# Gated linear attention into a two-layer feed-forward, one core: another order of the same work, and the last unit's second layer in two column halves

## The chip, the cores and the metric

The kernel runs on one core of one Trainium2 chip. The metric is the device time of one execution in microseconds (us). A core has five engines that run at once, each through its own list of instructions in the order of the program: TensorE (PE: matrix products; PEld is its weight load), VectorE (DVE), ScalarE (ACT), GpSimd (POOL) and SyncE (SP, which here only issues transfers). An instruction waits for others only through semaphores. While it waits, everything behind it on its engine waits too.

## The reference

The inputs are `q`, `k`, `v` and `f_logit`, each 4 batches x 8 heads x 768 steps x 48, and two weight matrices of 384 x 2048 and 2048 x 384, all in float32.

```python
f = 1.0 / (1.0 + np.exp(-f_logit))
for t in range(S):
    state = f[:, :, t, :, None] * state + np.einsum('bhd,bhe->bhde', k[:, :, t], v[:, :, t])
    y[:, :, t] = np.einsum('bhd,bhde->bhe', q[:, :, t], state)
...
x = np.ascontiguousarray(attn_out.transpose(0, 2, 1, 3)).reshape(B * S, H * D)
...
h = x @ w_in
g = np.maximum(0.01 * h, h)
return (g @ w_out).astype(np.float32)
```

## The kernel before, in words

The 768 steps are cut into 6 chunks of 128. A chunk of one batch is a *unit*, so there are 24 units; unit u is batch u % 4 of chunk u // 4. In a chunk the recurrence becomes matrix products: keys and queries are scaled by the exponentials of the summed gate logarithms, the scores of 128 x 128 steps are masked to their upper triangle, and the state of 48 x 48 for each head is carried from chunk to chunk. The 128 x 384 result of a unit is one row block of the feed-forward, whose first layer makes 16 blocks of 128 x 128 (`gT`) and whose second layer sums over them into 128 x 384.

The work is written as small steps, and a long list of calls at the end of the function sets the order. The scheduler of the framework is switched off (`ctx.enter_context(tc.manual_schedule())`, line 57). A step is put on its engine at the place where it is called, so each engine's list is the list of calls with the other engines' steps struck out. Eight PSUM banks of 128 x 512 float32 (`ps0` to `ps7`) are given by hand: the last number of most calls is the bank. A step that writes a bank waits for the step that last read it.

The steps that the prediction speaks of:

- Opening (chunk 0, names with `q_`): `q_exp_act` and `q_ln_act` (ACT, lines 222 and 225) make the gate's logarithm of one half of the heads each; `q_gate32` (PE, L233) sums it over time; `q_decay_b` (ACT, L238) takes exponentials into `gT3` and `gT4`, which are lent for it; `q_turn_pe`, `q_k_mul`, `q_q_mul` (PE L262, DVE L267) transpose and scale keys and queries; `q_score_pe` (PE L281) makes scores; they are masked on DVE (`q_mask`, L292) or copied by ACT (`q_wf_act`, L285) and selected by POOL (`q_mask_pool`, L288); `q_mix_pe` (PE L307) applies them to the values. `idle_pe` (L140) are matrix products of zeros that only keep PE running.
- From chunk 1 on: `g_exp`, `g_ln` (ACT, L337, L341), `g_sum` (DVE, L345), `g_cast` (POOL or DVE), `g_pe` (PE, L352 and L355), `g_add` (DVE, L361), `g_em`, `g_a` (ACT, L365, L369), then `g_k` and `g_q` (DVE, L377), which scale two heads each. In chunk 1 keys and queries are transposed on PE (`t_pe`, L408) and copied out by ACT or DVE (`t_out`); from chunk 2 or 3 on by transposing transfers (`t_dma`, L401) after `kq_dma` (L396) has laid them out. `cast_v` and `v_dma` (L391) bring the values.
- `score_pe` (PE, L420), `mask` (DVE, L424), `mix_pe` (PE, L432 and L436), `x_out` (copy to the first layer's input), `state_pe` (PE, L444), `state_dve` (DVE), `state_pool` (POOL), and for chunk 0 `q_state_dve` (L323) and `q_state_pool`, whose two casts are L329.
- First layer: `up` (PE, L468; chunk 0, two units at a time, six matrix products of 256 columns) and `up4` (L478; four units, three of 512 columns), each followed by `up_act` or `up4_act` (ACT, L473, L482). Second layer: `down(u, part, bank)` (PE, L486), four of the sixteen products of 384 columns; after part 3 `put` copies the bank to SBUF and `out_dma` or `outs_dma` (L502, L505) sends it out.
- `load_all` (SP, L73) brings 768 KB of one input; `load_w_in` and `load_w_out` (POOL, L181 and L186) bring a quarter of a weight matrix and cast it to bf16 on the way. `gate`, `touch` and `clear` are small writes; a transfer into a tile that `gate` has touched waits for it.

Two helpers stand in the kernel before without being called; the change calls them:

```python
def down_cols(u, c0, bk):
    for ff in range(NF):
        nc.tensor.matmul(bank(bk)[:, 0:KD // 2], g_part(u, ff),
                         w_out_b[:, ff, c0:c0 + KD // 2], start=(ff == 0), stop=(ff == NF - 1))

def put_cols(eng, u, c0, bk):
    move(eng, osbs[u // B % 2][:, u % B, c0:c0 + KD // 2], bank(bk)[:, 0:KD // 2])
```

Of the kernel before, what the change touches and what calls it, by code (L numbers as in the profile page):

```python
# [16 lines left out]
def kernel(  # L17
# [12 lines left out]
    B, H, S, D = q.shape  # L30
# [480 lines left out]
    clear(G, 'b')  # L511
    q_exp_act(0)
    clear(G, 'q')
    q_ln_act(0)
    q_exp_act(1)
    idle_pe(11, 7)
    q_gate32(0, 0, 1, 2, 3)
    gate(V, fqs[1])
    clear(V, 'v')
    load_all(fqs[1], f_logit, 1)  # L520
    q_ln_act(1)
    q_decay_b(1, emT, 1.0, 1, 0)
    idle_pe(9, 7)
    q_gate32(1, 0, 1, 2, 3)
    gate(G, fqs[0])
    q_k_cast(V, 1)
    q_decay_b(0, aT, -1.0, 0, 0)
    touch('k')
    load_all(fqs[0], f_logit, 2)
    gate(G, kqs[1])  # L530
    q_k_cast(V, 0)
    q_decay_b(3, emT, 1.0, 3, None)
    idle_pe(6, 7)
    q_turn_pe(khq, 0, 4)
    q_decay_b(0, emT, 1.0, 0, 0)
    q_decay_b(1, emT, 1.0, 1, 1)
    q_turn_pe(khq, 1, 5)
    q_decay_b(1, aT, -1.0, 1, 1)
    q_k_mul(0, 1, 0, 4)
    q_decay_b(0, emT, 1.0, 0, 1)  # L540
    q_decay_b(2, emT, 1.0, 2, None)
    q_q_cast(G, 1)
    q_k_mul(1, 1, 0, 5)
    q_k_mul(1, 0, 0, 5)
    q_decay_b(0, aT, -1.0, 0, 1)
    q_decay_b(2, aT, -1.0, 2, None)
    q_k_mul(0, 0, 1, 4)
    q_k_mul(0, 0, 0, 4)
    q_decay_b(1, aT, -1.0, 1, 0)
    q_q_cast(G, 0)  # L550
    idle_pe(12, 7)
    q_turn_pe(qhq, 1, 0)
    q_decay_b(3, aT, -1.0, 3, None)
    q_q_mul(1, 1, 0, 0)
    load_w_in(0)
    q_k_mul(1, 1, 1, 5)
    q_v_cast(A, 0)
    idle_pe(5, 7)
    q_turn_pe(qhq, 0, 3)
    q_k_mul(1, 0, 1, 5)  # L560
    q_k_mul(0, 1, 1, 4)
    order_pe(1)
    load_w_in(1)
    q_v_cast(A, 1)
    q_back_pe(1, 5)
    q_q_mul(1, 1, 1, 0)
    q_back_pe(2, 4)
    q_q_mul(1, 0, 1, 0)
    load_w_in(2)
    q_q_mul(0, 0, 1, 3)  # L570
    q_back_out(A, 2, 4)
    idle_pe(3, 7)
    q_score_pe(1, 1, 2, 6)
    q_q_mul(1, 0, 0, 0)
    q_wf_act(1, 1, 1, 6)
    q_q_mul(0, 0, 0, 3)
    idle_pe(3, 7)
    q_score_pe(1, 0, 0, 4)
    q_q_mul(0, 1, 1, 3)
    q_pick(2, 7)  # L580
    q_wf_act(1, 0, 1, 4)
    order_out(1)
    q_mask_pool(1, 1, 1)
    q_q_mul(0, 1, 0, 3)
    g_exp(1, 0)
    q_score_pe(0, 1, 1, 6)
    load_w_in(3)
    q_v_out(V, 2, 7)
    q_pick(3, 3)
# [772 lines left out]
```

## Time and profile before

| | us |
|---|---|
| median of three runs | 176.68 (176.44 to 177.47) |
| the profiled execution's own time | 176.75 |
| its span, from the first to the last recorded event | 175.1 |
| PE busy | 168.9 |
| ACT busy | 111.7 |
| DVE busy | 110.1 |
| POOL busy | 50.9 |

The profile is of one execution. Rows of the timeline give the start of a group of like instructions, how long it lasted, the engine, the source line, the operation, what it writes and reads, and how many there were; a bracket at the end gives the idle time of the engine before it and what ended it. Starts are in us from the span's start. A matrix product's recorded length includes its way through the array, so that the next one starts before it ends: costs on PE are read from start to start. Lines of helpers (L146 for a copy on ACT, L148 for one on DVE or POOL) are shared by many steps and told apart by their tiles.

### The profile page before, as it was taken

The numbers are of one execution on the slowest core, as the hardware profiler recorded it, in microseconds if no ns is written. First come the engines' busy times: TensorE is split into PE (matmuls) and PEld (weight loads), VectorE is DVE, ScalarE is ACT, GpSimd is POOL, SyncE is SP. The second block draws the span as 40 slices with busy tenths as digits, with TensorE's granted clock in tenths as the row PEclk, the third lists the DMA queues.
The fourth block names the chain that finished last, engine by engine and source line by source line (L and its number), as shares of the span: only waits on it lengthen the run. The fifth ranks groups of instructions, "written<-read, shape, count | busy, mean of one in ns | idle before, by whom it ended". The sixth has DMA issues, their size and how long they took to land.

```text
span 175.1 us, 4631 instructions
## 1 busy us (share of the span) xinstructions
PE 168.9 (96%) x1887; PEld 107.9 (62%) x1887; DVE 110.1 (63%) x228; ACT 111.7 (64%) x200; POOL 50.9 (29%) x101
## 2 busy tenths in 40 slices
PE   7999999989999999999999999999999999999991
PEld 5786698865665566655555655555755556555560
DVE  7959996998894989992747856796601763110000
ACT  2789999977059987876792299970368401472522
POOL 7565610483000872009520003460006610000000
PEclk9999999999999999999999999999999999999998
DMA  5999999996699997999997899875998880000234
GB/s 159 314 327 311 211 219 329 238 206 193 196 340 330 276 114 206 339 330 332 251 181 239 240 363 171 224 152 184 290 253 171 231 291 4 0 0 0 107 113 144
DMA packets 52773, 37.53 MB, mean 214 GB/s; under 512 B 16400, under 2 KB 52240, under 8 KB 52752
## 3 DMA queue, kind: packets, MB, share of 16 engines
q1 hardware_dynamic: 50016, 33.69, 70.3%
q0 software_dynamic: 2176, 3.15, 10.3%
q10 hardware_dynamic: 560, 0.39, 0.8%
q8 instruction: 15, 0.25, 0.6%
q14 instruction: 6, 0.05, 0.1%
HBM read 25.17 MB, written 4.72 MB: 171 GB/s over the span
## 4 chain that ended last, share of the span: by engine, by line
PE 85%; ACT 6%; DVE 6%; issue 1%
PE ps L486 34%; PE ps L478 30%; PE ps L140 5%; PE ps L420 3%; PE ps L436 3%; ACT gT L238 2%; PE ps L432 2%; DVE khQ L377 2%; PE ps L444 2%; ACT gT L473 2%; DVE fq L361 2%; PE ps L252 2%; PE ps L468 1%; ACT fq L341 1%; PE ps L281 1%
## 5 line engine op out<-in xcount | busy, mean ns | idle before, releaser
L486 PE MATMUL ps<-w_out_b,gT 128*128 128x384 bf16 x384 | 69.5, 326 | 0.0
L482 ACT ACTIVATE gT<-ps 128x512 bf16<-128x512 f32 x80 | 44.3, 604 | 20.8 <-PE ps L478 20.0
L478 PE MATMUL ps<-xQ,w_in 128*128 128x512 bf16 x240 | 57.1, 379 | 0.0
L486 PEld LDWEIGHTS <-gT 128*128 128x128 bf16 x384 | 36.2, 98 | 25.3
L478 PEld LDWEIGHTS <-w_in 128*128 128x128 bf16 x240 | 26.4, 114 | 20.5 <-issue 0.2
L424 DVE TENSOR_TENSOR wm<-ps,ut 128x512 bf16<-128x512 f32 x40 | 25.2, 684 | 6.3 <-PE ps L420 6.3
L146 ACT CAST xQ<-ps 128x384 bf16<-128x384 f32 x12 | 5.2, 480 | 25.5 <-PE ps L436 25.5
L458 POOL TENSOR_TENSOR sf<-sf,a_end 128x192 f32<-128x192 f32 x16 | 9.3, 583 | 37.6 <-DVE sf L453 37.0
L329 POOL CAST sb<-sf 64x192 bf16<-64x192 f32 x40 | 15.8, 395 | 2.3
L377 DVE TENSOR_TENSOR qhQ<-qq,a_t 128x384 bf16<-128x384 f32 x20 | 11.5, 589 | 4.6 <-DMA qq<-in_q_dram 2.2
L361 DVE TENSOR_TENSOR fq<-fq,ps 128x768 f32<-128x768 f32 x10 | 9.4, 953 | 6.5 <-PE ps L444 3.2
L377 DVE TENSOR_TENSOR khQ<-kq,em_t 128x384 bf16<-128x384 f32 x20 | 12.1, 638 | 1.8 <-ACT em_t L365 1.6
L140 PE MATMUL ps<-fill 128*128 128x256 bf16 x73 | 11.6, 321 | 1.1 <-DVE fill L97 1.1
L148 DVE COPY osb<-ps 128x384 f32<-128x384 f32 x10 | 5.4, 553 | 10.6 <-PE ps L486 10.4
L148 POOL CAST vQ<-v_raw 128x768 bf16<-128x768 f32 x8 | 7.3, 931 | 15.6 <-DMA v_raw<-in_v_dram 15.5
L468 PE MATMUL ps<-xQ,w_in 128*128 128x256 bf16 x96 | 11.5, 273 | 0.3 <-ACT gT L473 0.3
L148 POOL CAST lfq<-fq 128x384 bf16<-128x384 f32 x5 | 2.7, 547 | 27.8 <-DVE fq L345 16.3
L468 PEld LDWEIGHTS <-w_in 128*128 128x128 bf16 x96 | 10.1, 114 | 0.5 <-issue 0.4
L140 PEld LDWEIGHTS <-fill 128*128 128x128 bf16 x73 | 7.9, 115 | 3.3 <-DVE fill L97 1.1
L146 ACT COPY osb<-ps 128x384 f32<-128x384 f32 x14 | 6.6, 481 | 5.1 <-issue 3.3
L452 DVE TENSOR_TENSOR sf<-sf,ps 64x192 f32<-64x192 f32 x16 | 5.5, 344 | 6.7 <-PE ps L444 5.3
L345 DVE TENSOR_TENSOR fq<-fq 128x384 f32<-128x384 f32 x15 | 9.0, 599 | 1.0 <-ACT fq L341 0.7
(97 smaller groups left out, 195.9 us busy)
## 6 DMA issues: line engine op xcount, KB each, us to landing
kq<-in_k_dram SPq DMA_DIRECT2D x6, 768.0 KB, 6.9
qq<-in_q_dram SPq DMA_DIRECT2D x6, 768.0 KB, 7.3
fq<-in_f_logit_dram SPq DMA_DIRECT2D x5, 768.0 KB, 7.2
v_raw<-in_v_dram SPq DMA_DIRECT2D x5, 768.0 KB, 9.6
out_dram<-osb SPq DMA_DIRECT2D x4, 768.0 KB, 3.9
kh<-khQ SPq DMA_DIRECT2D x20, 128.0 KB, 4.9
v_b<-vQ SPq DMA_DIRECT2D x20, 128.0 KB, 2.2
w_in<-in_moe_w_in_dram POOLq DMA_DIRECT2D x4, 384.0 KB, 9.8
```

The costliest lines, as they stand in the source:

```text
L140: nc.tensor.matmul(bank(bk)[:, 0:256], fill[:, 0:128], fill[:, 0:256], start=True, stop=True)
L146: eng.copy(out=out, in_=in_)
L148: eng.tensor_copy(out=out, in_=in_)
L329: nc.gpsimd.tensor_copy(out=state_b[b][r, :, e * D:(e + 1) * D], in_=state_f[b][r])
L361: nc.vector.tensor_add(t, t, x[:, :, None, :].to_broadcast([128, 4, 4, D]))
L377: eng.tensor_mul(out.rearrange("p (j g) d -> p j g d", j=4)[:, :, h, 0:D], raw[:, h].rearrange("p e j d -> p j e d"), by[:, h].rearrange(" ...
L424: nc.vector.tensor_mul(wms[e][u % R_WM], bank(bk).rearrange("p (i n) -> p i n", i=P2), ut[:, None, :].to_broadcast([128, P2, 128]))
L458: nc.gpsimd.tensor_mul(sf, sf, a_ends[c % 2][:, :, b:b + 1].to_broadcast([128, P2, D]))
L468: nc.tensor.matmul(bank(bk)[:, i * 256:(i + 1) * 256].rearrange("p (a n) -> p a n", a=2), w_in_p[ff // 4][:, kk, :, ff % 4], xQs[0][:, 2 * ...
L478: nc.tensor.matmul(bank(bk).rearrange("p (a n) -> p a n", a=B), w_in_p[ff // 4][:, kk, :, ff % 4], xQs[c % R_XT][:, :, kk, :], start=(kk = ...
L482: nc.scalar.activation(g_piece(c, ff), bank(bk), AF.Prelu, alpha=0.01)
L486: nc.tensor.matmul(bank(bk)[:, 0:KD], g_part(u, ff), w_out_b[:, ff, :], start=(ff == 0), stop=(ff == NF - 1))
```

## The change

All steps stay as they are, but for the last unit's second layer; nearly the whole list of calls stands in another order, with other banks and other units first. One line of `cast_v` now names the buffer by a remainder, which with one buffer is the same buffer. What else differs in kind:

- The fill products (`idle_pe`) are 66, and were 73.
- In the opening one query cast moves from POOL to DVE, one value cast from ACT to POOL, one of the copies of `q_back_out` and one of `q_v_out` from ACT to DVE, one `clear` from POOL to DVE. Later one `t_out` moves from DVE to ACT, two `x_out` from DVE to ACT, and one `g_cast` from POOL to DVE.
- The last unit, 23, has no `down` steps. `down_cols` makes columns 192 to 383 in bank 1, then columns 0 to 191 in bank 7, each with sixteen products of 192 columns; each half has a `put_cols` and an `outs_dma` of its own.

```diff
     def cast_v(eng, c, hh):
         h = slice(4 * hh, 4 * hh + 4)
-        move(eng, vQ[:, :, h, 0:D], v_raws[0][:, h].rearrange("p h j d -> p j h d"))
+        move(eng, vQ[:, :, h, 0:D], v_raws[c % len(v_raws)][:, h].rearrange("p h j d -> p j h d"))
...
-    down(23, 3, 6)
-    down(21, 3, 0)
-    put(A, 23, 6)
-    down(22, 2, 7)
-    outs_dma(5, 3, 4)
-    put(A, 21, 0)
-    down(20, 3, 1)
-    outs_dma(5, 1, 2)
-    down(22, 3, 7)
-    put(A, 20, 1)
-    outs_dma(5, 0, 1)
-    put(A, 22, 7)
-    outs_dma(5, 2, 3)
+    down(21, 3, 7)
+    put(A, 20, 3)
+    down_cols(23, 192, 1)
+    outs_dma(5, 0, 1)
+    put(A, 21, 7)
+    outs_dma(5, 1, 2)
+    down_cols(23, 0, 7)
+    put_cols(A, 23, 192, 1)
+    outs_dma(5, 3, 4, 192, 384)
+    put_cols(A, 23, 0, 7)
+    outs_dma(5, 3, 4, 0, 192)
```

Three places of the new order, as they stand on the engines. Numbers after a tile's name tell its buffers apart (`ps0` is bank 0, `fq1` the gate of odd chunks).

ACT in the opening, from the two halves' exponentials on. Before:

```order
L222 ACTIVATE fq0_71<-fq0_71 128x768
L225 ACTIVATE lfq0_107<-fq0_71 128x16x48
L222 ACTIVATE fq0_71<-fq0_71 128x768
L225 ACTIVATE lfq1_108<-fq0_71 128x16x48
L238 ACTIVATE gT4_176<-ps1_62 128x2x128
L238 ACTIVATE gT3_175<-ps0_61 128x2x128
```

Now:

```order
L222 ACTIVATE fq0_71<-fq0_71 128x768 x2
L225 ACTIVATE lfq0_107<-fq0_71 128x16x48
L225 ACTIVATE lfq1_108<-fq0_71 128x16x48
L238 ACTIVATE gT4_176<-ps0_61 128x2x128
L238 ACTIVATE gT4_176<-ps1_62 128x2x128
```

Both exponentials now precede both logarithms, so no activation follows the one whose result it reads.

POOL while chunk 1 is made ready (`w_out_b` the second layer's weights, `vQ` the values, `sb` the four batches' states). Before:

```order
L148 CAST lfq0_107<-fq0_71 128x8x48
L186 DMA w_out_b_104<-in_moe_w_out_dram 128x1536 x3
L148 CAST vQ_157<-v_raw0_149 128x4x4x48 x2
L329 CAST sb2_123<-sf2_119 64x4x48 x2
L329 CAST sb1_122<-sf1_118 64x4x48 x2
```

Now:

```order
L148 CAST lfq0_107<-fq0_71 128x8x48
L186 DMA w_out_b_104<-in_moe_w_out_dram 128x1536
L329 CAST sb2_123<-sf2_119 64x4x48 x2
L329 CAST sb0_121<-sf0_117 64x4x48 x2
L329 CAST sb3_124<-sf3_120 64x4x48 x2
L186 DMA w_out_b_104<-in_moe_w_out_dram 128x1536 x2
L148 CAST vQ_157<-v_raw0_149 128x4x4x48 x2
L329 CAST sb1_122<-sf1_118 64x4x48 x2
```

Three of the four pairs of state casts now stand ahead of the value casts and of two weight loads.

SP from chunk 1's transfers to chunk 2's transposes (`kh1` the keys of chunk 1, `kh0` those of chunk 2, `kq1` and `qq1` the raw keys and queries of chunk 3). Before:

```order
L73 DMA kq0_73<-in_k_dram 128x8x192
L73 DMA fq1_72<-in_f_logit_dram 128x8x192
L73 DMA qq0_75<-in_q_dram 128x8x192
L73 DMA v_raw0_149<-in_v_dram 128x8x192
L396 DMA kh0_154<-khQ0_109 128x1x512 x4
L73 DMA fq0_71<-in_f_logit_dram 128x8x192
L401 DMA_TRANSPOSE kTs0_185<-kh0_154 128x8x128
```

Now:

```order
L73 DMA fq1_72<-in_f_logit_dram 128x8x192
L73 DMA kq0_73<-in_k_dram 128x8x192
L73 DMA qq0_75<-in_q_dram 128x8x192
L73 DMA v_raw0_149<-in_v_dram 128x8x192
L396 DMA kh1_155<-khQ1_110 128x1x512
L73 DMA kq1_74<-in_k_dram 128x8x192
L396 DMA kh0_154<-khQ0_109 128x1x512 x4
L73 DMA qq1_76<-in_q_dram 128x8x192
L401 DMA_TRANSPOSE kTs0_185<-kh0_154 128x8x128 x2
```

The chunk's keys are loaded second instead of first, and the raw keys and queries of chunk 3 and one layout transfer of chunk 1 now stand ahead of chunk 2's transposes.

More of the change, by code (lines that the diff above doesn't have):

```diff
@@ L656 @@
[L656 to L679 removed]
+    q_v_out(V, 0, 3)
+    state_pe(3, 2)
+    g_exp(2, 1)
@@ new lines @@
+    up_act(0, 5, 2)
+    load_w_out(1)
+    q_state_dve(1)
+    up_act(0, 4, 1)
+    g_pe(2, 6)
+    up(0, 6, 2)
+    up_act(1, 4, 3)
+    g_add(1, 0, 7)
+    up_act(0, 1, 4)
+    state_pe(2, 5)
+    up(1, 6, 3)
+    g_a(1, 1)
+    q_state_dve(0)
+    up(0, 7, 4)
+    g_a(1, 0)
+    q_state_dve(2)
+    down(3, 0, 0)
+    g_em(1, 0)
+    g_q(V, 1, 0)
+    q_state_pool(2)
+    down(2, 0, 5)
+    g_q(V, 1, 2)
+    up_act(1, 6, 3)
+    up(1, 7, 1)
+    g_end(1, 7)
+    q_state_pool(0)
+    up_act(0, 6, 2)
@@ L1080 @@
[L1080 removed]
+    up4(3, 9, 7)
     state_dve(13)
[L1082 to L1104 removed]
```

1436 lines of the change are left out of this document (704 added, 732 removed).

## The prediction

> **What bounds the kernel now.** I read the page first, then busy time by stretches, then PE's own rows wherever it waits, then what it waited for.
>
> ```profile
> span 175.1 us, 4631 instructions
> ```
>
> The profiled execution took 176.75 us, so 1.65 lie around its span; the median of 176.68 is 0.07 below it. I sum against 176.75.
>
> ```profile
> 42.00:171.40 129.40, 129.38 (x1405) 76.81 (x1399) 74.14 (x138) 76.06 (x138) 28.76 (x57) 1.00 0.77 204
> ```
>
> The columns are the stretch, its length, then busy us of PE, PEld, DVE, ACT and POOL, the clock and the transfers' share. From 42.00 to PE's end PE is busy for 129.38 of 129.40 us, at full clock. No other order of the same products can shorten that; it can only open a hole. What can be won lies ahead of 42 and after 171.4. Ahead of 42 PE's rows give the points that count:
>
> ```profile
> 20.91 0.34 PE L444 MATMUL ps<-v_b,kh 128*128 128x96 bf16 x4
> 21.09 0.39 PE L313 MATMUL ps<-ident,kTs 128*128 128x128 bf16 x4
> 21.40 0.63 PE L307 MATMUL ps<-wm,v_b 128*32 128x128 bf16 x32
> 21.97 2.81 PE L468 MATMUL ps<-xQ,w_in 128*128 128x256 bf16 x24
> ```
>
> ```profile
> 38.40 1.07 PE L408 MATMUL ps<-ident,khQ 128*128 128x128 bf16 x16 [0.67 <-DVE khQ L377]
> 39.30 2.11 PE L486 MATMUL ps<-w_out_b,gT 128*128 128x384 bf16 x12
> 41.73 0.62 PE L420 MATMUL ps<-qTs,kTs 64*128 64x128 bf16 x16 [0.31 <-DVE kTs L148]
> ```
>
> The feed-forward, which needs nothing but PE for most of its time, starts with the first layer's product at 21.97. Chunk 1's first scores start at 41.73; until then PE waits for scaled keys (the first bracket), then for their transposed copies (the second). At 41.73 seven `down` steps are done; twelve products begin at 39.30 and 0.163 each is what one costs (1.48 for the nine that end the program, below), so a step is 0.65.
>
> ```profile
> 169.92 1.48 PE ps L486 x9
> ...
> 171.42 0.48 ACT osb L146
> ```
>
> This is the end of the chain of waits: last products, a copy of 128x384, and then a transfer:
>
> ```profile
> GB/s 0 0 0 96 288 307 346 442 403 326 192 58 231 403 346 326 403 422 250 77 0 0 0 0 0 0 0 0 0 0 0 0 0 0 0 0 0 0 0 0
> ...
> out_dram<-osb SPq DMA_DIRECT2D x1, 192.0 KB, 1.9
> ```
>
> The columns of the first row are forty slices of 0.08 us from 171.8 on. Two bursts, the earlier output and the last one, each of some 0.6 us; the rest of the 1.9 is fixed.
>
> **Opening, to the first `up`.**
>
> ```profile
> 5.42 0.84 ACT L222 ACTIVATE fq<-fq 128x768 f32<-128x768 f32 x1 [1.89 <-DMA fq<-in_f_logit_dram]
> 6.29 0.84 ACT L225 ACTIVATE lfq<-fq 128x768 bf16<-128x768 f32 x1
> 7.04 0.83 ACT L222 ACTIVATE fq<-fq 128x768 f32<-128x768 f32 x1
> ...
> 9.80 4.00 ACT L238 ACTIVATE gT<-ps 128x256 f32<-128x256 f32 x11 [0.78 <-PE ps L233]
> ...
> 19.61 0.58 ACT L285 CAST wm<-ps 128x512 bf16<-128x512 f32 x1
> ```
>
> An activation that reads the one ahead starts 0.87 after it (5.42 to 6.29), another 0.75 after (6.29 to 7.04). With both exponentials first, the steps start at 5.42, 6.17, 6.92 and 7.67, and the second logarithm ends near 8.5 and not 8.75. The first gate sum is later, behind four more fill products (39 for 35), the second earlier; so the pause of 0.78 ahead of 9.80 shrinks, and I get the decays' end at 13.1 instead of 13.8. A value cast goes to POOL, so ACT is free at 14.05 instead of 15.2. That lead does not last: the copies behind it wait on PE's scores and DVE's masks, and walking the new order with these durations I find the last masked copy ending at 20.25, against 20.19 (19.61 + 0.58), and POOL's select, which follows, at 20.95:
>
> ```profile
> 20.27 0.63 POOL L288 TENSOR_SCALAR_AFFINE_SELECT wm<-wm 128x512 bf16<-128x512 bf16 x1 [0.57 <-ACT wm L285]
> ```
>
> So select and mask are no earlier. What changes is PE behind them: before, `state_pe` (20.91), the turn back (21.09) and 32 mix products (21.40, 0.57 to the next row) followed the select; now the first two stand ahead, and only the mix is left. First `up` at 20.95 + 0.57, some 21.55: **0.42 earlier**. Bounds: 0 if the select is 0.4 late, 0.6 if the two mixes merge with it better.
>
> The other casts that change engine (one query cast, `q_back_out`, `q_v_out`) and the `clear` are in this walk; none of them ends last ahead of a PE step there. If DVE is late by one 0.4 copy, the 0.42 is gone, which is the lower bound again.
>
> **From first `up` to chunk 1's scores.** ACT paces `up` and the gate, DVE the scaling.
>
> ```profile
> 26.29 1.60 ACT L341 ACTIVATE fq<-fq 128x768 f32<-128x768 f32 x2
> ...
> 29.45 1.12 ACT L473 ACTIVATE gT<-ps 128x512 bf16<-128x512 f32 x2
> ...
> 40.34 1.03 ACT L146 COPY kTs<-ps 128x1024 bf16<-128x1024 bf16 x1
> ```
>
> ```profile
> 34.11 0.96 DVE L377 TENSOR_TENSOR qhQ<-qq,a_t 128x384 bf16<-128x384 f32 x2
> 34.99 3.36 DVE L377 TENSOR_TENSOR khQ<-kq,em_t 128x384 bf16<-128x384 f32 x4
> 38.38 0.95 DVE L361 TENSOR_TENSOR fq<-fq,ps 128x768 f32<-128x768 f32 x1
> ```
>
> ```profile
> 35.40 1.92 POOL L148 CAST vQ<-v_raw 128x768 bf16<-128x768 f32 x2 [1.07 <-DMA v_raw<-in_v_dram]
> 37.27 3.68 POOL L329 CAST sb<-sf 64x192 bf16<-64x192 f32 x8
> ```
>
> ```profile
> L186 POOL DMA_DIRECT2D w_out_b<-in_moe_w_out_dram x3: 538/551/561, 32.7 to 33.8; - x3
> ...
> DMA to landing us min/median/max: 4.3/5.8/7.2
> ```
>
> ACT now runs seven activations of 768 (0.735 each, half of 26.29 to 27.76) from 20.57, then twelve `up_act` (0.48, half of 29.45 to 30.41) to 31.5, then two `g_a`, the last ending near 33.1. DVE follows with eight products. Two take 0.88 undisturbed (34.11 to 34.99). The four at 34.99 took 3.36 where 3 x 0.44 + 0.55 = 1.87 would do: 1.49 more, beside 2.95 us of POOL's casts (35.40 to 38.35), or 0.5 for each us of cast. Three pairs of state casts (0.46 a cast) now stand ahead of the value casts, so 4.3 us of casts, not 2.95, lie beside the eight products: 2.15 more. With one `g_add` of 0.95, the last keys come at 33.15 + 8 x 0.44 + 2.15 + 0.95 = 39.8. They then need 0.6 for PE's transposes and 1.03 for the copy, which now goes to ACT and no longer stands behind DVE's `g_add`: scores at 41.4 against 41.73, and with eight `down` steps done, not seven. PE's lead is 0.33 + 0.65 less 0.2 for the second scores' `g_add`: 0.78, of which 0.42 is the opening's. This stage: **0.36**. Ends for the stage: 0.9 gained if DVE loses a quarter of that drag, 0 if it loses a quarter more; a drag of 1 us for each us of cast is a rival below.
>
> In POOL's list the six state casts (2.8) also stand ahead of the weights' last two quarters. The third, issued second of the three at 33.25, landed at 39.06 (the median 5.8); 2.8 later would be 41.9. The eight `down` steps ahead of the scores use the first two quarters, and the ninth starts behind the scores, at 42.0. So it costs nothing if POOL reaches its loads no later than that; each us more is a us of PE, and I keep 0.3 of it in the stage's lower end.
>
> **The steady part.** Same products, in number and kind; nothing to win at 129.38 of 129.40, and 0 taken, if chunk 2's transposes come in time (rival).
>
> **The tail.** 32 products of 192 columns cost as much as 16 of 384 if columns decide: 2.6 either way. The four of 96 columns at 20.91, each with a weight tile of its own, take 0.18 to the next row, 0.045 each. The last copy is of 192 columns: 384 took 0.48 and 512 took 0.58 (the row at 19.61), 0.10 for 128 columns, so 0.33 for 192, **0.15 less**. The last transfer is half: of a burst of some 0.6 for 192 KB I take **0.2** (0 if the fixed part decides, 0.3 if the half counts in full). The other half's copy and transfer lie beside the last sixteen products. Sum of the tail 0.35.
>
> **Sum.** 0.42 + 0.36 + 0.35 = 1.13, so 175.6 us. Ends of all terms: 0.6 + 0.9 + 0.65 is 2.15, 174.6; 0 + 0 + 0.05 is 176.7, and 0.3 more with late weights 177.0.
>
> **Rivals.** First, the same side, no change that can be measured (within 0.5%, 0.9 us, which is about what a measurement of this kernel tells apart).
>
> ```profile
> 12.29 2.50 POOL L181 DMA_DIRECT2D w_in<-in_moe_w_in_dram  x3
> ...
> DMA to landing us min/median/max: 8.2/9.8/10.4
> ```
>
> The first quarter of `w_in` landed at 20.5 (12.29 + 8.2). It is now issued some 1.7 us later, behind a value cast on POOL. If landing follows issue, first `up` is at 22.2 and not 21.55: +0.65, 176.2. Against it:
>
> ```profile
> 12.00:16.00 4.00, 3.90 (x50) 3.08 (x49) 3.92 (x13) 3.91 (x9) 2.79 (x4) 1.00 1.10 328
> ```
>
> the transfers are saturated at that time, so the weights wait for the loads ahead rather than for their issue. 0.10. Or the products by halves are bound by their weight loads:
>
> ```profile
> L486 PEld LDWEIGHTS <-gT 128*128 128x128 bf16 x384 | 36.2, 98 | 25.3
> ```
>
> 32 of 98 ns are 3.1 where the columns need 2.6: +0.5, 176.1; the row at 20.91 speaks against it, 0.05. The Trainium skill's page "TensorE: Matmul & The Clock Gate", section "LDWEIGHTS (loading the stationary operand)", gives a load's time as columns over 1.2 ns, 107 for these tiles; an estimate by it is 3.4 for the tail, +0.8. The 98 of the row agrees with its size; the products of 96 columns at 20.91 started 0.045 apart, so here the loads did not set the pace. Last, the stage's gain may go in small losses between DVE and POOL: 176.4, 0.15.
>
> Slower. The queue of transfers may be late with chunk 2's transposes, on which PE would stand still.
>
> ```profile
> 46.00 1.77 SPq L73 DMA_DIRECT2D qq<-in_q_dram  x1
> 47.81 2.26 SPq L73 DMA_DIRECT2D v_raw<-in_v_dram  x1
> ```
>
> ```profile
> qq<-in_q_dram SPq DMA_DIRECT2D x1, 768.0 KB, 9.8
> v_raw<-in_v_dram SPq DMA_DIRECT2D x1, 768.0 KB, 10.4
> ```
>
> ```profile
> L401 SPq DMA_TRANSPOSE kTs<-kh x8: 1240/1313/2585, 59.0 to 132.8; - x8
> ...
> DMA to landing us min/median/max: 3.1/3.8/5.7
> ```
>
> ```profile
> 68.16 0.62 PE L420 MATMUL ps<-qTs,kTs 64*128 64x128 bf16 x16
> ```
>
> Loads landed at 55.8 and 58.2, 2.4 apart. In the new order one more load (2.4) and four layouts (128 KB, so 0.4 each by that pace) follow these, and another load stands ahead of the two transposes on SP. The layouts land near 58.2 + 2.4 + 1.6 = 62.2, the first transpose is issued then, the second 1.3 later, and with the median of 3.8 it lands at 67.3. PE needs it at 68.2 less its lead, 67.4. With the slow issue of 2.6 and the worst landing of 5.7 it is 62.2 + 2.6 + 5.7 = 70.5, 3.1 late: 178.7. It decides from 68.5 on, where the 1.13 are used up; three quarters of the way to the worst it is 2.3 late: 177.9. 0.13. For it: the margin is within one median transpose. Against: the loads need not be as slow, since fewer are on the way at once.
>
> Slower too, if POOL's casts stop DVE's products outright: 4.3 in place of 2.15 beside them, +2.15, since the `down` steps that could fill the time would still want the later quarters: 177.7. It needs 1 us lost for each us of cast and the row gave 0.5. 0.06. The Trainium skill's page "SBUF — State Buffer", section "Who interferes with whom", states such a rule: a VectorE instruction with two SBUF inputs and a GpSimd one that reads SBUF hold their shared ports in turn, the later wholly blocked. Over this stretch the trace, at 0.5, does not agree with it.
>
> **How the numbers follow.** 0.51 for the forecast (174.5 to 175.8, 175.6 likeliest), 0.30 for the same side (0.10 + 0.05 + 0.15, 175.8 to 177.5), 0.19 for slower (0.13 + 0.06). The range goes to 177.6, taking in the same side and the near part of the slower, and down to 174.5, the sum of the good ends. Faster by over 0.5% is under 175.8, 0.51; slower over 177.56, 0.19.
>
> **What the next profile would show.** First `up` near 21.55; four L377 products on `khQ` ending by 39.8 with fewer than 2.5 us lost beside casts; first scores near 41.4; a stretch from there to PE's end without idle time, above all none at 66 to 70; last copy of 192 columns near 0.33 and span end some 3.3 after PE's end, before 3.7. It would be wrong by a new bracket on the L420 rows from `kTs` and L401, by first `up` over 22, or by more than 2.7 us for the last 32 products.

## The result and the profile after

The changed kernel takes 175.86 us (median of 22 runs, 174.81 to 177.88) where the kernel before takes 176.68 (22 runs): a ratio of 0.9942, 95% interval 0.9923 to 0.9961. The forecast was 175.6, faster. The profiled execution took 176.12, 0.63 less than the one of before. Ratios, here and below, leave out the few executions that were over 1.5% above the fastest of their kernel; medians take in all. The forecast's total came out close, but none of its four terms came out at its size: the opening gave almost nothing, the stage to chunk 1's scores gave more than was forecast, the steady part lost, and the tail gave more. That these errors nearly cancel is luck, and what follows is about the terms.

The windows of the changed kernel, with columns as before:

```profile
22.00:42.00 20.00, 19.52 (x201) 16.64 (x200) 17.20 (x33) 18.63 (x32) 8.16 (x15) 1.00 1.02 233
42.00:171.30 129.30, 128.75 (x1403) 77.35 (x1403) 72.96 (x137) 76.71 (x140) 28.87 (x56) 1.00 0.78 209
```

Where the kernel before had 0.02 us of PE idle time behind 42, this one has 0.55. PE's timeline has the start of the first layer, the scores of chunk 1 and the three longest waits (the last, ahead of 60.20, is too short for a bracket in the view):

```profile
21.06 0.38 PE L140 MATMUL ps<-fill 128*128 128x256 bf16 x2
21.37 0.63 PE L307 MATMUL ps<-wm,v_b 128*32 128x128 bf16 x32
21.94 6.08 PE L468 MATMUL ps<-xQ,w_in 128*128 128x256 bf16 x54
...
39.52 0.62 PE L408 MATMUL ps<-ident,khQ 128*128 128x128 bf16 x8 [0.48 <-DVE khQ L377]
39.98 1.46 PE L486 MATMUL ps<-w_out_b,gT 128*128 128x384 bf16 x8
41.37 0.62 PE L420 MATMUL ps<-qTs,kTs 64*128 64x128 bf16 x16
...
52.68 1.46 PE L478 MATMUL ps<-xQ,w_in 128*128 128x512 bf16 x6
54.51 2.75 PE L478 MATMUL ps<-xQ,w_in 128*128 128x512 bf16 x12 [0.37 <-ACT osb L146]
...
59.80 0.25 PE L444 MATMUL ps<-v_b,kh 128*128 128x96 bf16 x2
60.20 0.32 PE L352 MATMUL ps<-lfq,before 128*128 128x384 bf16 x1
```

The first product of the first layer is at 21.94 and not at 21.55; it was at 21.97 before. The scores are at 41.37 (41.73 before, 41.4 forecast) with eight `down` steps done and not seven. With the eighth step's 0.65, PE is 1.01 ahead at its first scores. But PE ends at 171.29, 0.11 earlier only: about 0.9 was given back behind it. Idle time shows only 0.55 of this, since a product's recorded length reaches some 0.17 into each wait behind it. From start to start the waits cost 0.53 (six products of 0.217 from 52.68 on would let the next one start at 53.98, not 54.51) and 0.31 (at 60.20, where two of 0.043 each from 59.80 on would let it start at 59.89). The halves add 0.05.

The wait at 54 is for ACT's copy of a bank, and ACT's timeline says why that copy is late. The same exponential in the kernel before, then ACT in the changed kernel:

```profile
54.01 0.84 ACT L337 ACTIVATE fq<-fq 128x768 f32<-128x768 f32 x1
```

```profile
50.92 0.84 ACT L337 ACTIVATE fq<-fq 128x768 f32<-128x768 f32 x1 [0.66 <-DMA fq<-in_f_logit_dram]
51.67 0.46 ACT L146 COPY osb<-ps 128x384 f32<-128x384 f32 x1
52.03 0.84 ACT L365 ACTIVATE em_t<-fq 128x768 bf16<-128x768 f32 x1
52.77 0.83 ACT L337 ACTIVATE fq<-fq 128x768 f32<-128x768 f32 x1
53.51 0.58 ACT L482 ACTIVATE gT<-ps 128x512 bf16<-128x512 f32 x1
53.99 0.47 ACT L146 COPY osb<-ps 128x384 f32<-128x384 f32 x1
```

ACT waited until 50.92 for chunk 3's gates to land, and everything behind that exponential, the copy at 53.99 with it, moved. The gates are not late by the old measure: they are issued at 45.39 (45.32 before) and landed at 52.53 in the kernel before. What moved is their reader, from 54.01 to the place where ACT was free at 50.26. DVE waited for chunk 2's keys, which are now loaded behind those gates: issued at 46.08 and landed at 53.21, where it was 44.58 and 50.14. DVE's first product on them before, and now:

```profile
50.23 1.50 DVE L377 TENSOR_TENSOR khQ<-kq,em_t 128x384 bf16<-128x384 f32 x3
```

```profile
53.31 0.56 DVE L377 TENSOR_TENSOR khQ<-kq,em_t 128x384 bf16<-128x384 f32 x1 [1.03 <-DMA kq<-in_k_dram]
```

The tail, in the chain of waits and in the table of transfers:

```profile
168.63 2.65 PE ps L491 x32
171.29 0.02 issue
171.31 0.32 ACT osb L146
```

```profile
out_dram<-osb SPq DMA_DIRECT2D x1, 96.0 KB, 1.6
```

32 products of half the columns take 2.65, the copy 0.32, the transfer 1.6. From PE's end to the span's end it is 3.1 us and was 3.65 (175.05 less 171.40).

### The profile page after: what moved, and what is told of

It reads as the page before. It is cut to its first block, busy times and chain, and to the rows that moved or that the text cites. A ratio compares the mean times of both kernels' runs of the same rounds, so it can differ in the third digit from the quotient of the medians.

```text
span 174.4 us, 4660 instructions
## 1 busy us (share of the span) xinstructions
PE 168.3 (96%) x1896; PEld 108.4 (62%) x1896; DVE 109.2 (63%) x230; ACT 110.8 (64%) x201; POOL 49.9 (29%) x99
## 4 chain that ended last, share of the span: by engine, by line
PE 68%; ACT 9%; DMA 8%; DVE 7%; SPq 4%; issue 2%; POOL 0%; ACTq 0%; DVEq 0%
PE ps L486 29%; PE ps L478 24%; DMA qq<-in_q_dram 6%; ACT gT L473 3%; PE ps L420 3%; DMA fq<-in_f_logit_dram 2%; SPq L391 2%; PE ps L436 2%; PE ps L432 2%; PE ps L252 2%; PE ps L491 2%; DVE qhQ L377 1%; PE ps L444 1%; ACT fq L341 1%; ACT fq L337 1%
## 5 line engine op out<-in xcount | busy, mean ns | idle before, releaser
L486 PE MATMUL ps<-w_out_b,gT 128*128 128x384 bf16 x368 | 66.3, 326 | 0.0
L478 PE MATMUL ps<-xQ,w_in 128*128 128x512 bf16 x240 | 56.1, 379 | 0.4 <-ACT osb L146 0.4
L482 ACT ACTIVATE gT<-ps 128x512 bf16<-128x512 f32 x80 | 42.8, 611 | 17.2 <-PE ps L478 16.8
L486 PEld LDWEIGHTS <-gT 128*128 128x128 bf16 x368 | 34.4, 98 | 23.2
L146 ACT CAST xQ<-ps 128x384 bf16<-128x384 f32 x14 | 6.1, 482 | 21.1 <-PE ps L436 21.0
L329 POOL CAST sb<-sf 64x192 bf16<-64x192 f32 x40 | 17.5, 436 | 4.9 <-DVE sf L323 2.5
L146 ACT COPY osb<-ps 128x384 f32<-128x384 f32 (+1 forms) x15 | 6.8, 456 | 13.3 <-PE ps L486 8.6
L140 PE MATMUL ps<-fill 128*128 128x256 bf16 x66 | 10.3, 318 | 1.1 <-DVE fill L97 1.1
L148 POOL CAST lfq<-fq 128x384 bf16<-128x384 f32 x4 | 2.1, 529 | 29.1 <-ACT gT L482 16.6
L365 ACT ACTIVATE em_t<-fq 128x768 bf16<-128x768 f32 x10 | 8.7, 874 | 0.4 <-DVE fq L361 0.4
```

The source lines that it names most:

```text
L140: nc.tensor.matmul(bank(bk)[:, 0:256], fill[:, 0:128], fill[:, 0:256], start=True, stop=True)
L146: eng.copy(out=out, in_=in_)
L148: eng.tensor_copy(out=out, in_=in_)
L329: nc.gpsimd.tensor_copy(out=state_b[b][r, :, e * D:(e + 1) * D], in_=state_f[b][r])
L478: nc.tensor.matmul(bank(bk).rearrange("p (a n) -> p a n", a=B), w_in_p[ff // 4][:, kk, :, ff % 4], xQs[c % R_XT][:, :, kk, :], start=(kk = ...
L482: nc.scalar.activation(g_piece(c, ff), bank(bk), AF.Prelu, alpha=0.01)
```

## The experiments

Each run is set against the kernel before on the same chip. The intervals are some 0.3% wide to either side, as large as most single effects here, so verdicts rest on the profile where a median can't carry one. Columns: the ratio; the first product of the first layer; the first scores of chunk 1; PE's idle time from 42 to 165, in which each wait shows some 0.17 less than it costs; the start of the last copy. The kernel before took 176.49 to 176.66 (medians) beside the experiments.

| kernel | median | ratio (95%) | first `up` | scores | idle 42-165 | last copy |
|---|---|---|---|---|---|---|
| before | 176.68 | 1 | 21.97 | 41.73 | 0.00 | 171.42 |
| changed | 175.86 | 0.9942 (0.9923-0.9961) | 21.94 | 41.37 | 0.52 | 171.31 |
| changed, again | 176.10 | 0.9962 (0.9934-0.9989) | 21.80 | 41.10 | 0.82 | 171.51 |
| before, halves at the end | 176.10 | 0.9975 (0.9944-1.0006) | 21.82 | 40.80 | 0.35 | 171.17 |
| changed, last unit whole | 176.29 | 0.9989 (0.9960-1.0019) | 22.52 | 41.77 | 0.30 | 171.62 |
| keys ahead of gate sum | 175.51 | 0.9938 (0.9911-0.9964) | 22.18 | 40.97 | 0.03 | 170.59 |
| the two later waits | 176.34 | 0.9976 (0.9944-1.0008) | 21.99 | 41.48 | 1.44 | 172.52 |
| opening | 175.65 | 0.9945 (0.9919-0.9970) | 21.94 | 41.63 | 0.59 | 171.63 |
| keys and waits | 175.78 | 0.9959 (0.9928-0.9990) | 22.01 | 40.79 | 0.55 | 170.94 |
| state casts late | 176.97 | 0.9980 (0.9941-1.0020) | 22.50 | 41.28 | 2.62 | 173.55 |
| keys loaded first | 178.20 | 1.0079 (1.0047-1.0110) | 22.42 | 41.72 | 2.16 | 173.34 |
| fewer fills | 175.80 | 0.9948 (0.9921-0.9976) | 22.32 | 41.41 | 0.42 | 171.42 |
| four moves | 175.23 | 0.9937 (0.9908-0.9966) | 21.71 | 40.69 | 0.00 | 169.80 |
| four moves, again | 175.42 | 0.9915 (0.9878-0.9952) | 21.48 | 40.47 | 0.00 | 169.61 |

**The tail alone, both ways.** First the kernel before with its own last unit in two halves:

```diff
-    down(22, 0, 7)
...
-    down(22, 1, 7)
...
-    down(22, 2, 7)
...
-    down(22, 3, 7)
...
-    put(A, 20, 1)
-    outs_dma(5, 0, 1)
-    put(A, 22, 7)
-    outs_dma(5, 2, 3)
+    down_cols(22, 192, 7)
+    put(A, 20, 1)
+    outs_dma(5, 0, 1)
+    down_cols(22, 0, 6)
+    put_cols(A, 22, 192, 7)
+    outs_dma(5, 2, 3, 192, 384)
+    put_cols(A, 22, 0, 6)
+    outs_dma(5, 2, 3, 0, 192)
```

> The kernel before with nothing changed but its last unit (22 there): its four steps are taken out and two column halves stand at the end, each with its copy and transfer. Theory: the halves cost PE nothing, the last copy shrinks from 0.48 to 0.32 and the last transfer from 1.9 to 1.6, so the time falls by 0.4 to 0.5 us (ratio 0.997 to 0.998) and PE's last 32 products take 2.65. Rival (the weight loads set the pace): 32 x 98 ns, PE ends 0.5 later and the time is unchanged.

Then the changed kernel with its last unit whole:

```diff
-    down_cols(23, 192, 1)
+    down(23, 0, 1)
+    down(23, 1, 1)
...
-    down_cols(23, 0, 7)
-    put_cols(A, 23, 192, 1)
-    outs_dma(5, 3, 4, 192, 384)
-    put_cols(A, 23, 0, 7)
-    outs_dma(5, 3, 4, 0, 192)
+    down(23, 2, 1)
+    down(23, 3, 1)
+    put(A, 23, 1)
+    outs_dma(5, 3, 4)
```

> The changed kernel with the last unit's second layer whole again, one copy and one transfer. Theory: the tail is worth 0.4 to 0.6 of the change, so this is 176.3 where the changed kernel is 175.8, and from PE's end to the span's end it is 3.6 again, not 3.1. Rival (the gain lies all in the order): no difference from the changed kernel.

The chain of waits of the first:

```profile
168.49 2.65 PE ps L491 x32
171.15 0.02 issue
171.17 0.32 ACT osb L146
```

and of the second, with its last transfer:

```profile
171.59 0.02 issue
171.62 0.48 ACT osb L146
```

```profile
out_dram<-osb SPq DMA_DIRECT2D x1, 192.0 KB, 1.9
```

From PE's end to the span's end it is 3.1 with halves (span 174.28, PE's end 171.15) and 3.6 whole (175.22, 171.59); 3.1 and 3.65 were the figures of the two kernels themselves, so the order of the rest does not matter. So the tail is worth about 0.5 in the trace, and the 32 products cost 2.65 in both, 0.083 each, where the prediction's row gave 0.098 for a weight load: the loads do not bound the halves. In the times, the tail alone gives a ratio of 0.9975 and the order alone 0.9989; both intervals hold 1, and the two together make the 0.9942 within their widths. The tail is the part that the traces show each time; of the new order alone a gain isn't shown.

The first kernel taught something else. Up to chunk 5 it is the kernel before, instruction by instruction, yet its scores of chunk 1 are at 40.80 and not 41.73. So a term read off one profile in the first 42 us carries up to 0.9 of the execution's own spread. The scaling of the keys and POOL's value casts show where the 0.93 is made; this is the first kernel, and the prediction has the same two rows of the kernel before (34.99 and 35.40):

```profile
34.84 2.58 DVE L377 TENSOR_TENSOR khQ<-kq,em_t 128x384 bf16<-128x384 f32 x4
```

```profile
35.87 2.24 POOL L148 CAST vQ<-v_raw 128x768 bf16<-128x768 f32 x2 [1.69 <-DMA v_raw<-in_v_dram]
```

The last key ends at 37.42 here and at 38.35 there, and from there to the scores it is 3.38 in both. Here the products began 0.15 earlier, and the values landed half a us later, so that only the last of the four products met a value cast and took 1.18. In the kernel before two products met one (1.18 and 1.17) and a third a state cast (0.69). And here too the lead was not kept: PE waited at 126.49 for DVE's copy of a bank (0.35 by its bracket), and the last copy started 0.25 earlier only.

**Chunk 1's last keys ahead of a gate sum.**

```diff
-    g_add(2, 0, 6)
+    g_k(V, 1, 2)
...
-    g_k(V, 1, 2)
+    g_add(2, 0, 6)
```

> The changed kernel with the last scaling of chunk 1's keys ahead of the gate sum that precedes it on DVE. Theory (DVE's product and POOL's cast take turns, one for one, whatever their lengths): the product runs at 37.5 before the first value cast starts at 38.2, takes 0.55 and not 1.07, the keys are ready at 38.1 and not 39.5, PE's hole of 0.64 ahead of their transposes goes, and the time falls by 0.4 to 0.6. Rival (the next wait takes its place: the gate sum, now later, holds the second score or a later step): the hole reappears behind 41 and the time is the same.

DVE in the changed kernel, and then in this one:

```profile
35.86 1.63 DVE L377 TENSOR_TENSOR khQ<-kq,em_t 128x384 bf16<-128x384 f32 x3
37.52 0.95 DVE L361 TENSOR_TENSOR fq<-fq,ps 128x768 f32<-128x768 f32 x1
38.40 1.07 DVE L377 TENSOR_TENSOR khQ<-kq,em_t 128x384 bf16<-128x384 f32 x1
```

```profile
36.11 2.10 DVE L377 TENSOR_TENSOR khQ<-kq,em_t 128x384 bf16<-128x384 f32 x4
38.24 0.95 DVE L361 TENSOR_TENSOR fq<-fq,ps 128x768 f32<-128x768 f32 x1
```

The fourth product is done at 38.2 and not 39.5, and PE's wait for keys is gone. The scores come at 40.97 although the opening was 0.24 later in this execution, and PE's idle time behind 42 fell to 0.03 (from start to start 0.2 is still lost at 54, where it was 0.53). The loads on SP tell why: SP's layout transfers of chunk 1's keys wait for the fourth product and start at 38.24, where they started at 39.49, and all that is issued behind them moves up with them. Chunk 3's gates are issued at 43.68 and not at 45.39, ACT waits for them 0.31 and not 0.66, and DVE for the keys 0.58 and not 1.03. The last copy starts 0.7 earlier than in the changed kernel. The median, 175.51, is 0.35 lower, but beside the kernel before on its own chip the ratio is 0.9938 where the changed kernel has 0.9942 and 0.9962: the times don't separate the two.

**The two later waits, by order alone.**

```diff
-    g_exp(3, 0)
...
-    up4_act(1, 3, 6)
-    state_dve(7)
     put(A, 1, 7)
+    state_dve(7)
     up4(1, 4, 4)
     up4_act(1, 5, 2)
+    g_exp(3, 0)
+    up4_act(1, 3, 6)
...
+    down(6, 0, 3)
     g_pe(3, 4)
...
-    down(6, 0, 3)
```

> The changed kernel with its two later PE waits taken away by order alone: ACT copies unit 1's bank out, and one first-layer activation, ahead of an exponential and another activation (the wait of 0.54 near 54); and one step of the second layer stands ahead of chunk 3's gate sum on PE (the wait of 0.31 near 60). Theory (what was gained by 42 was given back here): the time falls by 0.7 to 0.85 against the changed kernel, to 175.0. Rival (PE would only wait a little later for the same ACT): the same time as the changed kernel, with the idle time at another place.

The rival's outcome came, idle time at another place and no lower time, but not for the same ACT. PE did not wait at 54 and 60, but at 56 (1.21), and DVE's timeline tells for what:

```profile
55.38 0.56 DVE L377 TENSOR_TENSOR khQ<-kq,em_t 128x384 bf16<-128x384 f32 x1 [2.99 <-DMA kq<-in_k_dram]
55.97 0.34 DVE L452 TENSOR_TENSOR sf<-sf,ps 64x192 f32<-64x192 f32 x1
```

Chunk 2's keys landed at 55.3 in this execution (53.2 in the changed kernel's), and the state step behind the product that waits for them held a bank that PE wanted. So with ACT's copies out of the way, it is the landing of the keys that gives the lead back. Its size is not typical: the profiled execution took 177.35, 1.0 above the median of this kernel, and why the keys took 8.8 from issue to landing in it, and 7.1 in the changed kernel's, no run here tells.

**Which of the two loads.** Chunk 2's keys ahead of chunk 3's gates, as in the kernel before:

```diff
-    load_all(fqs[1], f_logit, 3)
+    load_all(kqs[0], k, 2)
...
-    load_all(kqs[0], k, 2)
+    load_all(fqs[1], f_logit, 3)
```

> The changed kernel with chunk 2's keys loaded ahead of chunk 3's gates again. Theory (one queue, 2.4 us a load): the keys land near 50.8 and not 53.2, DVE's first product of chunk 2 no longer waits for them; the gates land near 53.2, and ACT, whose exponential of chunk 3 stood at 50.9, waits for them with two copies of PSUM banks behind it, so that PE stands still near 53 to 55 for 1 to 2 us: 176.5 to 177.5. Rival (the keys are what costs): the hole near 60 goes, the time is 0.3 lower.

The theory held in place: keys at 50.68, gates at 53.10, and PE's waits behind ACT. The time came out 0.7 above its range. ACT:

```profile
53.21 0.84 ACT L337 ACTIVATE fq<-fq 128x768 f32<-128x768 f32 x1 [2.61 <-DMA fq<-in_f_logit_dram]
53.95 0.46 ACT L146 COPY osb<-ps 128x384 f32<-128x384 f32 x1
```

ACT's exponential starts 2.3 later, PE stands still twice behind ACT's copies (2.16 in all from 42 on), and the median is 178.20. DVE's first product did not gain from the early keys: it waited until 55.19 for an exponential that ACT has behind the one of the gates. The changed list of ACT needs the gates first, and even so it waits for them; issued near 45, behind the value transfers, the two loads are late for both their readers, and with the keys first ACT's wait grows from 0.66 to 2.61.

**The keys, and four moves around the waits.** The edit of chunk 1's last keys and that of the two later waits together, and the state step of unit 7 ahead of `g_k(V, 2, 3)` on DVE.

> The changed kernel with four moves: chunk 1's last keys ahead of the gate sum; unit 1's bank copied out earlier on ACT, with one exponential later; the state step of unit 7 on DVE ahead of the first product that waits for chunk 2's keys; one second-layer step ahead of chunk 3's gate sum on PE. Theory (the holes near 38, 54, 56 and 60 come from these four waits, and chunk 2's keys, loaded second, are the late thing behind two of them): PE has under 0.4 of idle time from 42 on, and the time is 1.0 to 1.5 below the changed kernel, 174.5. Rival (the keys' landing then stops something else): idle time between 55 and 66 of over 0.6 again, and 175.3 or more.

The scores came at 40.79, and PE then waited for weights:

```profile
41.38 2.12 PE L486 MATMUL ps<-w_out_b,gT 128*128 128x384 bf16 x12
43.83 0.81 PE L486 MATMUL ps<-w_out_b,gT 128*128 128x384 bf16 x4 [0.32 <-DMA w_out_b<-in_moe_w_out_dram]
```

That is the weights' last quarter, issued behind six state casts on POOL and landed at 43.78. In the changed kernel it landed at 43.00, 0.9 ahead of its first use; with the scores 0.6 earlier it comes late. The rest of the idle time, 0.23 at 62.10, is not behind late loads: PE waits there for a scaled query that stands on DVE behind chunk 3's gate sum. The time, 175.78, is the rival's; its idle time between 55 and 66 (over 0.6) is not what came, nor is the theory's total of under 0.4 (0.55).

**State casts behind the value casts.**

```diff
-    q_state_pool(2)
...
-    q_state_pool(0)
...
-    q_state_pool(3)
...
+    q_state_pool(2)
+    q_state_pool(0)
+    q_state_pool(3)
     q_state_pool(1)
```

> The changed kernel with the six state casts back behind the value casts on POOL, so that nothing of POOL's lies beside the first seven scaling products. Theory (a product and a cast take turns one for one: beside a state cast a product takes 0.62 from start to start, alone 0.46): five products win 0.15 each, the seventh ends near 36.7 and not 37.5, the gate sum and the last product then stand at 36.8 and 37.7, the last one still partly beside a value cast or clear of it; PE's wait ahead of the last transposes shrinks by 0.6 to 1.3, and the time by 0 to 0.6, less what the later states cost. Rival (a cost of 0.5 us for each us of cast, as forecast): the seven products lose 1.5 us to 3 us of casts, so they end near 36.0. A third: the mixes wait for the later states and the time is longer.

The time is no measure of the products here: POOL's value casts waited until 42.66 for the values, behind three weight loads that had gone out in a row, and all transfers behind them slid. But the profile shows the products alone, and so what a cast beside them costs. From the first start to the seventh end it is 3.37 (34.08 to 37.45) and was 3.96 (33.53 to 37.49): 0.6 won, near the theory's 0.75 and far from the rival's 1.5. Durations (least, median and most, in ns) of DVE's eight products in the kernel with late casts, then in the changed one:

```profile
L377 DVE TENSOR_TENSOR qhQ<-qq,a_t x4: 551/552/557, 34.1 to 35.5; 128x384 bf16<-128x384 f32 x4
L377 DVE TENSOR_TENSOR khQ<-kq,em_t x4: 550/551/552, 36.0 to 38.4; 128x384 bf16<-128x384 f32 x4
```

```profile
L377 DVE TENSOR_TENSOR qhQ<-qq,a_t x4: 558/694/701, 33.5 to 35.2; 128x384 bf16<-128x384 f32 x4
L377 DVE TENSOR_TENSOR khQ<-kq,em_t x4: 546/620/1067, 35.9 to 38.4; 128x384 bf16<-128x384 f32 x4
```

and POOL's casts beside the latter:

```profile
32.81 3.34 POOL L329 CAST sb<-sf 64x192 bf16<-64x192 f32 x6 [2.55 <-DVE sf L323]
...
38.23 1.92 POOL L148 CAST vQ<-v_raw 128x768 bf16<-128x768 f32 x2 [1.08 <-DMA v_raw<-in_v_dram]
```

A product lasts 0.55 alone, 0.69 beside state casts and 1.07 beside a value cast (up to 1.18 before). So in these rows the price goes with the length of the single cast that a product meets, and not with the us of casts in the stretch.

**The opening.**

```diff
-    q_v_out(A, 3, 6)
-    q_mask_pool(1, 0, 1)
     q_wf_act(0, 0, 1, 2)
+    q_mask_pool(1, 0, 1)
+    q_v_out(A, 3, 6)
...
-    idle_pe(2, 1)
     q_mix_pe(1, 3)
```

> The changed kernel with ACT's last masked copy of the opening ahead of a value copy, and without the two fill products between the state step and the last two mixes. Theory (POOL's last select, behind that copy, sets the first product of the first layer): the copy starts at 19.6 and not 19.9, the select ends near 20.8 and not 21.2, the first product starts near 21.65 and not 21.95, and the end is 0.2 to 0.3 earlier. Rival (the lead is only passed on to ACT, which paces the activations behind it): first product earlier, scores of chunk 1 at 41.4 as before, same time.

The select ended 0.3 earlier, but the first product stood at 21.94 again, since the scores themselves came 0.2 later in this execution. From the first scores of the opening to the first product it is 6.34 here and in both profiles of the four moves below, 6.54 or 6.55 in all nine with the opening as changed, and 6.52 in both with the opening of before. So the 0.2 is won, as expected, and hidden in the spread, and the change itself won nothing between these two points. The scores of chunk 1 gained nothing.

The spread has a cause that PE's first rows show, of the changed kernel, and of the one with its last unit whole, which has the same opening:

```profile
1.13 6.51 PE L140 MATMUL ps<-fill 128*128 128x256 bf16 x39 [1.13 <-DVE fill L97]
7.81 0.62 PE L233 MATMUL ps<-steps,lfq 32*128 32x128 bf16 x32 [0.17 <-ACT lfq L225]
```

```profile
1.13 7.21 PE L140 MATMUL ps<-fill 128*128 128x256 bf16 x39 [1.13 <-DVE fill L97]
8.27 0.62 PE L233 MATMUL ps<-steps,lfq 32*128 32x128 bf16 x32
```

The same 39 fills took 6.51 in one execution and 7.21 in the other. In the first the gate sum waited for ACT's logarithm, in the second for the fills. Nine profiles have these 39 fills ahead of it. In four the gate sum waited for the logarithm, and the opening's first scores came 9.94 to 9.99 after the first exponential; in five it stood behind the fills, and they came after 10.28 to 10.72. In two of the five, the one shown among them, PE waited for chunk 0's queries as well, so the fills are not the whole of it. 4 of them were taken out:

```diff
-    idle_pe(15, 7)
+    idle_pe(11, 7)
     q_gate32(0, 0, 1, 2, 3)
```

> The changed kernel with 11 in place of 15 fill products ahead of the opening's first gate sum. Theory (in about half of the executions PE is still busy with fills when ACT's first logarithm is ready, so the opening's length hangs on them): the first gate sum starts within 0.1 of the logarithm's end, near 7.7, the first product of the first layer comes 16.4 to 16.5 after the first exponential's start, where it came 16.5 to 17.3 before, and the median falls by 0.2 to 0.4. Rival (the fills lie beside other work): the first product where it was, the same median.

The gate sum started at 7.90, 2.36 after the first exponential, as in the first profile of the changed kernel; but the first product came 16.78 after it, not 16.5: chunk 0's queries landed at 11.45 there (10.98 in the changed kernel), and PE's transposes stood behind them. The median, 175.80, is not told apart from 175.86. Whether the fills cost anything in the median isn't settled.

**Four moves.** The keys ahead of the gate sum, the opening's edit, the fills, and the weights' loads spread between the state casts:

```diff
     q_state_pool(2)
...
+    load_w_out(2)
     q_state_pool(0)
...
+    load_w_out(3)
     q_state_pool(3)
...
-    load_w_out(2)
...
-    load_w_out(3)
```

> The changed kernel with 11 in place of 15 fills, the last masked copy of the opening ahead of a value copy and the two later fills left out, chunk 1's last keys ahead of the gate sum on DVE, and the second layer's last two weight loads spread ahead of the second and third pair of state casts on POOL. Theory (each removes one wait of its own): first product 16.2 after the first exponential, chunk 1's scores near 40.5, no wait on weights behind them, and a median of 174.6 to 175.2. Rival (the transfers of chunk 2 then bind, since they are issued behind the same value transfers): PE waits of 0.5 to 1 us between 42 and 62, and 175.5.

> The kernel of the four moves once more, unchanged. Theory (the four waits are really gone): a median of 174.8 to 175.4, ratio 0.990 to 0.994, and no PE wait between 42 and PE's end in a second profile either. Rival (the profile without waits was a lucky one): waits of 0.5 us or more behind the scores, and the ratio of the changed kernel, 0.994 to 0.997.

And the changed kernel beside it:

> The changed kernel as it is, again, for the spread of its profile and as a base for its neighbours here. Theory: a median of 175.6 to 176.0 (ratio 0.994 to 0.997), from PE's end to the span's end 3.1, waits of PE at the same places (ahead of the last key transposes, near 54, near 60) but of other lengths, with the first product between 21.9 and 22.5. Rival (the profile shown is typical to a tenth): first product at 21.94 and the same three waits within 0.1.

The windows of the second profile of the four moves:

```profile
22.00:42.00 20.00, 19.85 (x201) 16.83 (x200) 17.26 (x34) 18.37 (x32) 7.68 (x15) 1.00 1.07 255
42.00:169.00 127.00, 127.00 (x1395) 76.49 (x1392) 72.44 (x136) 76.59 (x140) 28.67 (x56) 1.00 0.79 209
```

No idle time behind 42, in both profiles, and the last copy starts 1.5 to 1.7 earlier than in the changed kernel. The first product came 16.3 after the first exponential, where 16.2 was expected, and the scores at 40.69 and 40.47. ACT's exponential of chunk 3 in the first profile:

```profile
49.50 0.84 ACT L337 ACTIVATE fq<-fq 128x768 f32<-128x768 f32 x1
```

It no longer waits: the gates landed at 48.97 and the keys at 51.35, ahead of their readers. What each of the four moves adds to this was not separated.

The medians are 175.23 and 175.42, against 176.10 for the changed kernel in the first of these two sets; the ratios 0.9937 and 0.9915 both lie in the 0.990 to 0.994 that the second run's theory gave, and the medians lie 0.03 and 0.02 above the upper side of what was expected. Both intervals of this kernel lie below 1, so it is faster than the kernel before; that it is faster than the changed kernel stands in the traces, while the intervals of the times overlap. The changed kernel's second profile has the same waits at 39, 54 and 60, of 0.35, 0.56 and 0.18 by its brackets, and its first product at 21.80, earlier than expected; its median is 0.1 above the expected range.

## Why the prediction was right, and where not

- *Total.* 1.13 was forecast; the profiles gave 0.63, the medians 0.82, the ratio 1.02 (0.0058 of 176.68). Right in sign and near in size, but close to the line that the prediction draws between faster and the same side, 175.8 or 0.5%: the median of 175.86 is 0.06 above it, and the ratio's interval (0.9923 to 0.9961) holds 0.995. Term by term the profiles give 0.03 + 0.98 - 0.90 + 0.53 = 0.64 where 0.42 + 0.36 + 0 + 0.35 was added up; the sum came near by luck.
- *Opening, 0.42.* It failed, with 0.03. The step that failed is "First `up` at 20.95 + 0.57". The select ended at 21.22, 0.27 later than walked, and the two fills that the list holds ahead of the last mix were not counted: they ran at 21.06, and the mix began at 21.37. The state step and the turn back did move ahead of it, as said, and brought nothing. The stretch of 6.54 or 6.55 against 6.52 above says the same in every profile.
- *Stage to chunk 1's scores, 0.36.* Scores at 41.37 against 41.4, with eight steps done: the place agrees, the term does not. Counted as the prediction counts it, PE's lead was 0.36 + 0.65 = 1.01 and not 0.78 (the 0.2 for the second scores was not lost: they come 3.26 behind the first, 3.25 before), and the opening's share is 0.03 and not 0.42, so the stage's is 0.98. Against the other profile with the list of before, where scores came at 40.80, the whole lead is 0.08 (40.80 + 0.65 - 41.37): the term was not something that one profile of before could carry. Inside it, the drag of POOL's casts was mis-sized: 2.15 us at 0.5 for each us of cast; in the profile it was 0.14 for each of four products beside state casts and 0.52 for the one beside a value cast, 1.1 in all. That the scores came where they were forecast all the same is luck: the products began 0.38 later than walked (33.53 for 33.15), took 0.47 each alone where 0.44 was used, and from the last key to the scores it was 1.9 (39.47 to 41.37) where 1.63 was taken. The weights' last quarters landed in time, as forecast: the third at 41.18 for its use at 41.92.
- *Steady part, 0.* It failed, with about 0.9 lost: 0.53 and 0.31 from start to start in the waits at 54 and 60, and 0.05 in the halves. "If chunk 2's transposes come in time" was the wrong condition: they came in time, the second landing at 67.8 (67.3 forecast) for scores at 69.2. What the condition left out is one step earlier, the raw loads: chunk 3's gates and chunk 2's keys are issued behind the value transfers near 45, and ACT and DVE wait for them, with work for PE's banks behind each. The keys land 3.1 later than before, second in the queue; the gates are issued when they were, and their reader on ACT moved up by more than 3. So in the slower rival a shift of the queue was right for the keys and the victim wrong, and a reader that moves up ahead of its load was not thought of. The kernels with the keys scaled earlier, and with the four moves, in which the loads are issued 1.5 to 1.7 earlier, lose little of this time or none.
- *Tail, 0.35.* The mechanism held, the size was 0.53: 0.16 from the copy, as forecast, 0.3 from the transfer where 0.2 was taken, the upper bound, and the rest, under 0.1, stands between PE's end and the span's end without a row of its own. The ends that went into the sum for this term, 0.05 and 0.65, are not the 0.15 and 0.45 that its two parts give; what was measured is above 0.45.
- *Rivals.* First weights late: the first quarter was issued at 14.2 and landed at 20.7, 0.2 later than before, no matter for PE; landing did not follow issue. Weight loads as the bound of the halves: 2.65, not 3.1, and not the 3.4 estimated with the 107 ns of the Trainium skill's page "TensorE: Matmul & The Clock Gate", section "LDWEIGHTS (loading the stationary operand)". POOL stopping DVE outright: the single rows show turns. A product and a state cast alternate, one for one: products start at 34.01, 34.63, 35.25 and 35.86, casts at 34.35, 34.97 and 35.59, 0.62 apart, where a product alone takes 0.47 from start to start and a cast 0.40. The Trainium skill's page "SBUF — State Buffer", section "Who interferes with whom", states that the shared ports are an exclusive lock and that the order of issue decides who blocks. The turns agree with it, against the sentence in the prediction that the trace does not; but a pair takes less than a product and a cast one behind the other (0.62 against 0.87), so the trace does not show that the later one is blocked for the whole of the other. What was wrong was the price worked out for it, 1 us for 1 us: at most one cast lies in the way of a product, and the next cast then stands behind the product.
- *Signs.* Of the signs of being wrong that the prediction names none came: no bracket on the scores' rows, the first `up` under 22, 2.65 for the last 32 products. What it said the profile would show and did not is the first `up` near 21.55 and the stretch without idle time.

## What to carry to other kernels

Where the bound engine is already busy without a gap, a new order can win nothing in that stretch; it can only lose there what it won ahead of it. So follow a lead to the next load that must land for it, and look what stands behind the instruction that waits. When a queue or a reader is moved, check every reader of each load in turn, raw loads first, not only the last link of the chain. Add the terms up afterwards, too: a total that comes out can hide terms that do not. And take two profiles of the kernel before, where terms are below half a us: their difference says which terms can be forecast at all.

## What the hardware showed that was not expected

The fills at the program's start do not run at one pace. Windows of PE, in the changed kernel with its last unit whole and in the second run of the four moves, from 4 to 6 us:

```profile
4.00:6.00 2.00, 2.00 (x11) 1.40 (x10) 1.96 (x9) 0.57 (x1) 1.15 (x2) 1.00 1.04 262
```

```profile
4.00:6.00 2.00, 2.00 (x18) 1.66 (x17) 1.96 (x9) 0.80 (x2) 1.14 (x2) 1.00 1.04 290
```

11 products lie in these two microseconds in one and 18 in the other, at a granted clock of 1.00 in both. The 39 fills lasted from 6.29 to 7.32 us in nine profiles; why, no run here tells.
